# Attention scores in fp32 without an fp16 split, heads always paired, some exponentials kept in SBUF: a fused attention and mixture-of-experts kernel

## The chip, the cores and the metric

The kernel runs on one core of one Trainium2 chip. The metric is device time in microseconds (us). Three timed runs of the kernel before gave a median of 1721.32 us (1719.0 to 1721.88). One more execution was recorded by the hardware profiler; all rows below come from it.

## The reference

Rotary attention feeds a dense mixture of experts with a Sinkhorn-normalised gate:

```python
B, H, S, D = 4, 8, 576, 64
q_rot, k_rot = rotate(q), rotate(k)                  # half = 32, cos/sin tables [S, 32]
scores = (1/sqrt(D)) * q_rot @ k_rot.T
scores -= max(scores, -1); attn = exp(scores)
attn /= sum(attn, -1) + 1e-9
x = (attn @ v) as [2304, 512]
P = exp(x @ w_gate - max); 8 times: normalise rows, then columns
out = sum over 8 experts of P[:, e] * (relu(x @ w1[e]) @ w2[e])   # 512 -> 1024 -> 512
```

## The kernel before

The 32 heads form 16 pairs: one head on partitions 0 to 63, the other on 64 to 127. A stage of attention over the 16 pairs comes first, with the first blocks of expert 0 slipped between; then a short stage with the gate, the Sinkhorn rounds and the rest of expert 0; then experts 1 to 7 as one long stream of matmuls (line 1096).

Attention, for each pair. POOL rotates q and k (lines 369, 373) and scales them by a power of two (385); DVE finds the largest magnitude first (`qk_max`, 282) and makes the scales (`qk_scale`, 350). ACT rounds to fp16 (`z_hi`, 381), POOL subtracts for a low half (`z_lo`, 391). The result is `Z`, four fp16 pieces, in three buffers. A unit is 128 query rows of one head against 576 keys; a pair has nine (four times two, and one "tail", i = 2, that packs 64 rows of both heads). TensorE (PE) multiplies three fp16 products per unit (`s_mm`, 443) into a PSUM tile of two banks; there are three such tiles (`ps_s`). Then, per unit: DVE takes the row maximum (`m_max`, 447), ACT scales it (451) and takes the exponential in place in PSUM with a row sum (454), DVE inverts the sum (458, 460), ACT writes the high fp16 half (`e_hi`, 463), DVE the low half (`e_lo`, 285), and only then is the PSUM tile free. SP transposes the halves by DMA (479, 475) and PE multiplies with v (`av_mm`, 490); ACT and DVE evacuate x (499, 501).

In the first eight pairs (SOLO = 8) each head's unit has score matmuls of its own; in the last eight the two heads' matmuls alternate. `Plan` orders the work: every operation has an engine, a due time (AT, SH1), a cost (US), dependencies and buffers. `Plan.run` plays these through and emits each engine's instructions in that fixed order; semaphores hold them back on the chip. Expert 0's chunks (F1, line 624; F2, line 645) have late due times, so on PE they fill gaps. They may be placed before the end of attention for three of five blocks (E0_IN); the rest waits for the score tiles' PSUM (`rel`).

Of the kernel before, what the change touches and what calls it, by code (L numbers as in the profile page):

```python
# [9 lines left out]
F32 = mybir.dt.float32  # L10
# [8 lines left out]
P = 128  # L19
# [24 lines left out]
SOLO = 8  # L44
# [5 lines left out]
E_TOP = 10  # L50
# [165 lines left out]
def attention_moe(ctx, tc, qk, v, trigs, eye, wg, w1, w2, out):  # L216
# [79 lines left out]
    trig = att.tile([P, 2, S], F32, name="trig")  # L296
# [50 lines left out]
    def qk_scale(p):  # L347
        s, inv = pow2_of(raw[p][2][:, 0:2], 2, 14, "p")
        c = small.tile([P, 1], F32, tag="pc", bufs=4, name="pc")
        dve.tensor_scalar(c, inv[:, 0:1], 1.0 / math.sqrt(D), inv[:, 1:2], op0=ALU.mult, op1=ALU.mult)  # L350
        sc[p] = (c, s)

    def qk_max(p):
        mx = small.tile([P, 2], BF16, tag="pmx", name="pmx")
        absmax(mx, raw[p][0])
        raw[p].append(mx)

    def qk_gmax(p):

        ps = ps_g.tile([P, 512], F32, tag="g", name="g")  # L360
        pe.matmul(ps[:, 0:2], neg, raw[p][2], start=True, stop=True)
        raw[p][2] = ps

    def rope_mult(e, p, n, t):
        r = raw[p][n]
        if t is None:
            engine[e].tensor_tensor(r, r, trig[:, n, :].unsqueeze(1).to_broadcast([P, 2, S]), op=ALU.mult)
        else:
            engine[e].tensor_tensor(r[:, t, :], r[:, t, :], trig[:, n, :], op=ALU.mult)
# [5 lines left out]
    def z_hi(p, t):  # L375
        if p not in Z:
            Z[p] = att.tile([P, 4, S], F16, tag="Z", bufs=ZB, name="Z")
        if p == 0:
            hi_of(Z[p][:, 2 * t, :], raw[p][0][:, t, :], sc[p][1][:, t : t + 1])
        else:  # L380
            act.copy(Z[p][:, 2 * t, :], raw[p][0][:, t, :])

    def z_scale(p, t, e):
        x = raw[p][0][:, t, :]
        engine[e].tensor_scalar(x, x, sc[p][1][:, t : t + 1], None, op0=ALU.mult)

    def z_lo(p, t, e="dve"):
        if p == 0:
            stt_lo(Z[p][:, 2 * t + 1, :], raw[p][0][:, t, :], sc[p][1][:, t : t + 1], Z[p][:, 2 * t, :])
        else:  # L390
            engine[e].tensor_tensor(Z[p][:, 2 * t + 1, :], raw[p][0][:, t, :], Z[p][:, 2 * t, :], op=ALU.subtract)
        if t == 1:
            del raw[p]

    def prep0():

        qk_max(0)
        qk_gmax(0)
        for t in range(2):
            rope_mult("dve", 0, 0, t)  # L400
        qk_scale(0)
        rope_mult("pool", 0, 1, 1)
        rope_mult("dve", 0, 1, 0)
# [25 lines left out]
    def s_mm(n, ps, js):  # L429

        p, i = divmod(n, 5)
        zz = Z[p]
        for j in js[:1] if i == TAIL else js:
            ps[j] = ps_s.tile([P, 2, 512], F32, tag="s", name="s")
        for x, y in ((0, 2), (1, 2), (0, 3)):
            for kh in range(2):
                for j in js:
                    r = HEADS[j]
                    if i == TAIL:
                        o, q = ps[0][r, kh, 0:HS], zz[r, x, 256:320]  # L440
                    else:
                        o, q = ps[j][:, kh, 0:HS], zz[r, x, QT[i] : QT[i] + P]
                    pe.matmul(o, q, zz[r, y, QH[kh]], start=(x, y) == (0, 2), stop=(x, y) == (0, 3))  # L443
# [5 lines left out]
    def e_exp(p, ps, b):  # L449
        c = small.tile([P, 1], F32, tag="nb", bufs=4, name="nb")  # L450
        act.activation(c, b[0], AF.Copy, bias=E_TOP * math.log(2.0), scale=sc[p][0])
        b.append(small.tile([P, 1], F32, tag="es", bufs=4, name="es"))
        e = ps[:, :, 0:HS]
        act.activation(e, e, AF.Exp, bias=c, scale=sc[p][0], accum_out=b[1])

    def e_inv(b):
        t = small.tile([P, 1], F32, tag="et", bufs=2, name="et")
        dve.tensor_scalar(t, b[1], 2.0**-N_TOP, 1e-9 * 2.0 ** (E_TOP - N_TOP), op0=ALU.mult, op1=ALU.add)
        b.append(small.tile([P, 1], F32, tag="ei", bufs=6, name="ei"))
        dve.reciprocal(b[2], t)  # L460

    def e_hi(n, ps, b):
        act.activation(ets[n % NEB][:, 0, 0:S].rearrange("p (a b) -> p a b", a=2), ps[:, :, 0:HS], AF.Copy, scale=b[2])  # L463

    def e_lo(n, ps, b):
        h, l = (ets[n % NEB][:, x, 0:S].rearrange("p (a b) -> p a b", a=2) for x in range(2))
        stt_lo(l, ps[:, :, 0:HS], b[2], h)
# [185 lines left out]
    def batch_logits(b):  # L653
# [3 lines left out]
        raw=2, Z=ZB, S=3, G=2, E=NEB, ET0=1, ET1=1, vraw=1, vhl=2, hA=1, hB=1, raw0=1, pc=4,  # L657
# [33 lines left out]
    def pair_ops(p):  # L691
# [7 lines left out]
        rw, z = ("raw", p), ("Z", p)  # L699
        if p > 0:  # L700
            add("ld", "sp", "ld", lambda: load_qk(p), allocs=[rw])
            add("mx", "dve", "mx", lambda: qk_max(p), ["ld"], uses=[rw])
            g = ("G", f"q{p}")
            add("gm", "pe", "gm", lambda: qk_gmax(p), ["mx"], allocs=[g])
            add("sc", "dve", "sc", lambda: qk_scale(p), ["gm"], allocs=[("pc", p)], uses=[g])
            for t, x in enumerate("qk"):
                add("z" + x, choice("ts", "tsd"), 0, lambda e, t=t: z_scale(p, t, e), ["a" + x, "sc"], uses=[rw])
                add("c" + x, choice("pro", "tt"), 0, lambda e, t=t: rope_mult(e, p, 0, t), ["mx"], uses=[rw])
                add("s" + x, choice("pro", "tt"), 0, lambda e, t=t: rope_mult(e, p, 1, t), ["ld"], uses=[rw])
                add("a" + x, choice("ad_p", "ad"), 0, lambda e, t=t: rope_add(p, t, e), ["c" + x, "s" + x], uses=[rw])  # L710
            add("hq", "act", "hi", lambda: z_hi(p, 0), ["zq"], allocs=[z], uses=[rw])
            add("hk", "act", "hi", lambda: z_hi(p, 1), ["zk", "hq"], uses=[z, rw])
            add("lq", choice("ptt", "tt"), 0, lambda e: z_lo(p, 0, e), ["hq"], uses=[z, rw])
            add("lk", choice("ptt", "tt"), 0, lambda e: z_lo(p, 1, e), ["hk", "lq"], uses=[z, rw])
        for h in range(2):
            plan.add(f"et{h}.{p}", ("none", 0.0), at["TR"], lambda: None, allocs=[(f"ET{h}", p)])
        for i in range(5):
            n, ps = 5 * p + i, {}
            solo = p < SOLO and i != TAIL
            for js in ((0,), (1,)) if solo else ((0, 1),):  # L720
# [3 lines left out]
                    ([f"lk.{p}"] if p else []) + before, allocs=[("S", (n, j)) for j in (js[:1] if i == TAIL else js)] + ([z] if n == js[0] == 0 else []),  # L724
                    uses=[z],
                )
                before[:] = [name]
            for j in range(1 if i == TAIL else 2):
                u, bb = 2 * i + j - (i > TAIL), []
                m = 9 * p + u  # L730
                pt, e = ("S", (n, j)), ("E", m)
# [698 lines left out]
```

## Time and profile before

| | |
|---|---|
| median of 3 runs | 1721.32 us |
| profiled execution | 1726.83 us, span 1725.0 us |
| last attention output (line 501) starts | 459.69 us |
| first matmul of experts 1 to 7 | 556.97 us |
| busy share of the span | PE 92%, DVE 81%, ACT 65%, POOL 40% |

The span runs from the first to the last instruction; 1.83 us of the profiled time lie around it. A busy share is an average over three stages that differ, so the rows below are taken by stage. PEclk is the granted TensorE clock as a share of full speed (2.4 GHz).

### The profile page before, as it was taken

What the parts mean: (1) busy time and instruction counts of PE and PEld (TensorE: products, weight loads), DVE (VectorE), ACT (ScalarE), POOL (GpSimd) and SP (SyncE); (2) the same over time, 40 slices, a digit from 0 to 9 for tenths busy, and PEclk for the clock granted to TensorE, in tenths of its full rate; (3) what the DMA queues carried; (4) which work ended last, traced back from release to release, by engine and by line L of the source; (5) the groups of instructions that cost most, each with busy time, mean ns of one, the idle gap of its engine ahead of it and who ended that gap; (6) DMA issues with size and microseconds to landing.
All of it is one profiled execution on the core that took longest, in us unless ns stands there. A gap on an engine that the chain in (4) does not pass through costs nothing.

```text
span 1725.0 us, 36197 instructions
## 1 busy us (share of the span) xinstructions
PE 1595.5 (92%) x14206; PEld 1271.9 (74%) x14206; DVE 1400.3 (81%) x2834; ACT 1119.5 (65%) x2320; POOL 693.6 (40%) x564
## 2 busy tenths in 40 slices
PE   3777776879999899999999999999999999999998
PEld 1444433444445798989898989898998989898987
DVE  7778876776698788888888888888888888887877
ACT  5678777677434866666666666666676666666643
POOL 5989879820135222223332322333232332332310
PEclk9856778899999999999999999999999999999999
DMA  8798977868412355646465556464655655555543
GB/s 259 147 192 188 226 157 142 176 102 121 94 55 94 116 153 139 153 122 164 117 156 130 146 129 159 113 158 123 155 131 145 136 146 149 142 143 131 135 115 95
DMA packets 243131, 243.67 MB, mean 141 GB/s; under 512 B 195600, under 2 KB 195728, under 8 KB 238864
## 3 DMA queue, kind: packets, MB, share of 16 engines
q1 hardware_dynamic: 224240, 180.01, 38.9%
q0 software_dynamic: 18720, 61.35, 19.9%
q8 instruction: 111, 1.82, 0.4%
q14 instruction: 60, 0.49, 0.1%
HBM read 123.36 MB, written 9.44 MB: 77 GB/s over the span
## 4 chain that ended last, share of the span: by engine, by line
PE 70%; DVE 2%; ACT 1%; issue 1%; POOLq 0%; DVEq 0%
PE m L1096 65%; PE g L645 3%; PE g L624 2%; ACT accA L883 0%; DVE prob L868 0%; DVE prob L859 0%; DVE hl L635 0%; ACT h L1137 0%; ACT accB L883 0%; DVE cs L866 0%; DVE accB L1159 0%; DVE u L1148 0%; PE g L490 0%; DVE h L1141 0%; DVE ts L916 0%
## 5 line engine op out<-in xcount | busy, mean ns | idle before, releaser
L1096 PE MATMUL m<-w2h,h 128*128 128x256 f16 x3528 | 627.2, 273 | 3.3 <-DVE accB L1159 1.5
L1096 PEld LDWEIGHTS <-h 128*128 128x128 f16 x5292 | 515.3, 98 | 63.5 <-issue 2.0
L1096 PE MATMUL m<-w2l,h 128*128 128x256 f16 x1764 | 480.8, 273 | 0.0
L1096 PEld LDWEIGHTS <-w1h 128*128 128x128 f16 x3920 | 369.2, 98 | 39.9 <-issue 3.0
L1096 PE MATMUL m<-ts,w1h 128*128 128x256 f16 (+1 forms) x2240 | 347.6, 262 | 2.7 <-ACT m L1119 1.3
L1161 ACT ACTIVATE ev<-m,pp 128x256 f32<-128x256 f32 x468 | 198.0, 468 | 186.2 <-PE m L1096 185.2
L1096 PE MATMUL m<-ts,w1l 128*128 128x256 f16 (+1 forms) x1120 | 284.0, 262 | 0.0
L1096 PE MATMUL m<-xx,w1h 128*128 128x256 f16 (+1 forms) x1680 | 261.4, 262 | 0.0
L1046 POOL TENSOR_TENSOR wraw<-wraw 128x512 f32<-128x512 f32 x112 | 160.7, 1435 | 176.1 <-issue 133.4
L1141 POOL TENSOR_TENSOR h<-u,h 128x512 f16<-128x512 f32 (+1 forms) x70 | 78.2, 1117 | 356.2 <-ACT h L1137 356.2
L1096 PE MATMUL m<-xx,w1l 128*128 128x256 f16 (+1 forms) x840 | 213.1, 262 | 0.0
L1096 PEld LDWEIGHTS <-w1l 128*128 128x128 f16 x1960 | 191.8, 98 | 17.8
L443 PE MATMUL s<-Z 64*128 64x288 f16 (+1 forms) x960 | 139.1, 361 | 65.3 <-DVE et L285 42.7
L1159 DVE SCALAR_TENSOR_TENSOR ev<-m,pp,ev 128x256 f32<-128x256 f32 x351 | 154.7, 478 | 45.4 <-ACT ev L1161 28.3
L443 PEld LDWEIGHTS <-Z 64*128 64x128 f16 (+1 forms) x960 | 70.4, 117 | 144.5 <-DVE et L285 60.6
L1137 ACT ACTIVATE h<-m 128x512 f16<-128x512 f32 (+1 forms) x210 | 120.4, 574 | 44.2 <-PE m L1096 40.7
L447 DVE TENSOR_REDUCE nm<-s 128x1 f32<-128x576 f32 x144 | 104.4, 752 | 44.2 <-PE s L443 43.4
L1122 DVE TENSOR_TENSOR u<-m,u 128x512 f32<-128x512 f32 (+1 forms) x140 | 88.9, 635 | 55.0 <-PE m L1096 29.2
L1137 ACT ACTIVATE h<-u 128x512 f16<-128x512 f32 (+1 forms) x210 | 122.4, 586 | 14.8 <-DVE u L1148 11.1
L285 DVE SCALAR_TENSOR_TENSOR et<-s,ei,et 128x576 f16<-128x576 f32 x144 | 114.0, 812 | 15.2 <-ACT et L463 14.8
L1119 ACT COPY u<-m 128x512 f32<-128x512 f32 (+1 forms) x140 | 75.9, 542 | 71.4 <-PE m L1096 70.4
L1170 POOL DMA_DIRECT2D accA<-ev x78 | 69.0, 1021 | 126.5 <-ACT ev L1161 108.4
(148 smaller groups left out, 2727.4 us busy)
## 6 DMA issues: line engine op xcount, KB each, us to landing
ts<-xd SPq DMA_DIRECT2D x110, 512.0 KB, 3.9
accA<-ev POOLq DMA_DIRECT2D x78, 512.0 KB, 5.9
wraw<-in_w SPq DMA_DIRECT2D x28, 1024.0 KB, 5.0
raw<-in_qk SPq DMA_DIRECT2D x32, 576.0 KB, 4.9
accB<-ev POOLq DMA_DIRECT2D x26, 512.0 KB, 7.3
ts<-xd SPq DMA_DIRECT2D x28, 256.0 KB, 2.9
accB<-ev POOLq DMA_DIRECT2D x26, 256.0 KB, 3.3
vraw<-in_v SPq DMA_DIRECT2D x4, 1280.0 KB, 7.2
```

What stands on the lines that cost most here:

```text
L285: dve.scalar_tensor_tensor(lo, x, s, hi, op0=ALU.mult, op1=ALU.subtract)
L443: pe.matmul(o, q, zz[r, y, QH[kh]], start=(x, y) == (0, 2), stop=(x, y) == (0, 3))
L447: dve.tensor_reduce(b[0], ps[:, :, 0:HS], axis=AX.XY, op=ALU.max, negate=True)
L1046: put(k, "pool", US["ptt"], lambda: pool.tensor_tensor(quad(o), quad(x), quad(y), op=op), deps, uses=[raw])
L1096: pe.matmul(live[bank][:, f_ * width : (f_ + 1) * width], step(x, i, f_), y[:, i], start=first and f_ == 0 and n == 0, stop=n == 5, skip_g ...
L1119: act.copy(live[n], live[src])
L1122: dve.tensor_tensor(live[n], live[x], live[n], **add)
L1137: act.activation(t[:, 0:cols], live[src], func)
L1141: engine[eng].tensor_tensor(l, live[src], h, **sub)
L1159: dve.scalar_tensor_tensor(o, x, s, o, op0=ALU.mult, op1=ALU.add)
L1161: act.activation(o, x, AF.Copy, scale=s)
L1170: pool.dma_start(out=a, in_=ev[th][:, 0:nt], accum_op=ALU.add)
```

## The change

Rotated q and k are no longer split. The score matmuls take the fp32 rows, once per unit and key half. The factor 1/8 goes into a second table `trigq` for q. Row maximum, exponential and sum need no scale any more. All pairs alternate heads (SOLO = 0). In units 0, 2, 5 and 7 of nine (`EU`) the exponentials go to one of four fp32 tiles in SBUF (`e32`), so their PSUM tile is free after the exponential; the five others stay in PSUM as before. Three rotated x tiles (`rx`) replace the three `Z`. The planner's costs change with it (`s` 0.9 to 1.3, `s8` 0.76 to 1.1, `ex`, `eh`, `tsv`, `tsw` up, `plv`, `plw` down); due times stay.

```diff
-SOLO = 8
+SOLO = 0
+EU = (0,2,5,7)
+E32 = 4
...
     def s_mm(n, ps, js):
-        zz = Z[p]
+        x = raw[p][0]
...
-        for x, y in ((0, 2), (1, 2), (0, 3)):
-            for kh in range(2):
-                for j in js:
...
-                    pe.matmul(o, q, zz[r, y, QH[kh]], start=(x, y) == (0, 2), stop=(x, y) == (0, 3))
+        for kh in range(2):
+            for j in js:
...
+                pe.matmul(o, q, x[r, 1, QH[kh]], start=True, stop=True)
...
-        c = small.tile([P, 1], F32, tag="nb", bufs=4, name="nb")
-        act.activation(c, b[0], AF.Copy, bias=E_TOP * math.log(2.0), scale=sc[p][0])
...
-        act.activation(e, e, AF.Exp, bias=c, scale=sc[p][0], accum_out=b[1])
+        if out:
+            b.append(att.tile([P, 2, HS], F32, tag="e32", bufs=E32, name="e32"))
+        act.activation(b[2] if out else e, e, AF.Exp, bias=b[0], accum_out=b[1])
...
-            add("mx", "dve", "mx", lambda: qk_max(p), ["ld"], uses=[rw])
-            add("gm", "pe", "gm", lambda: qk_gmax(p), ["mx"], allocs=[g])
-            add("sc", "dve", "sc", lambda: qk_scale(p), ["gm"], allocs=[("pc", p)], uses=[g])
...
-            add("hq", "act", "hi", lambda: z_hi(p, 0), ["zq"], allocs=[z], uses=[rw])
...
+                sb = u in EU
+                p2 = ("e32", m) if sb else pt
```

On DVE, in a late pair of the kernel before, a round of two units (score tiles s_3768 and s_3769) stands like this; `nm` is the maximum, `et_`/`ei_` the inverse, line 285 the low half:

```order
L447 TENSOR_REDUCE nm_3788<-s_3768 128x1
L447 TENSOR_REDUCE nm_3795<-s_3769 128x1
L282 TENSOR_REDUCE vmx_3804<-vraw_3666 128x1
L458 TENSOR_SCALAR et_3818<-es_3799 128x1
L460 RECIPROCAL ei_3820<-et_3818 128x1
L282 TENSOR_REDUCE vmx_3804<-vraw_3666 128x1
L458 TENSOR_SCALAR et_3831<-es_3816 128x1
L460 RECIPROCAL ei_3833<-et_3831 128x1
L285 SCALAR_TENSOR_TENSOR et3_101<-s_3768,ei_3820,et3_101 128x576
L282 TENSOR_REDUCE vmx_3804<-vraw_3666 128x1
L285 SCALAR_TENSOR_TENSOR et4_102<-s_3769,ei_3833,et4_102 128x576
L447 TENSOR_REDUCE nm_3875<-s_3853 128x1
```

The next round's maximum (s_3853) comes after both low halves of this one. On DVE of the changed kernel, in a middle pair, rounds s_2717/s_2718 and s_2777/s_2778:

```order
L402 TENSOR_REDUCE nm_2741<-s_2717 128x1
L402 TENSOR_REDUCE nm_2749<-s_2718 128x1
L415 TENSOR_SCALAR et_2773<-es_2758 128x1
L417 RECIPROCAL ei_2775<-et_2773 128x1
L415 TENSOR_SCALAR et_2784<-es_2771 128x1
L417 RECIPROCAL ei_2786<-et_2784 128x1
L402 TENSOR_REDUCE nm_2793<-s_2777 128x1
L402 TENSOR_REDUCE nm_2797<-s_2778 128x1
L592 SCALAR_TENSOR_TENSOR hl_2668<-g_2702,hh_2667 128x512
L285 SCALAR_TENSOR_TENSOR et1_100<-s_2718,ei_2786,et1_100 128x576
```

The next round's maxima now come ahead of the low half of s_2718. Over the whole order a round's first maximum stands ahead of the last low half of the round before it in 66 of 79 cases; before it was 37 of 40 in pairs 0 to 7 and 8 of 39 in pairs 8 to 15.

On PE of the kernel before, the start of one paired round of scores (12 matmuls, each with a weight load):

```order
L443 LDWEIGHTS Z_3469
L443 MATMUL s_4140<-Z_3469 128x288
L443 LDWEIGHTS Z_3469
L443 MATMUL s_4141<-Z_3469 128x288
L443 LDWEIGHTS Z_3469
L443 MATMUL s_4140<-Z_3469 128x288
L443 LDWEIGHTS Z_3469
L443 MATMUL s_4141<-Z_3469 128x288
```

And the end of one in the changed kernel, three of its four fp32 matmuls, with the first rows of the multiplication by v behind them:

```order
L398 MATMUL s_2718<-raw_2117 128x288
L398 MATMUL s_2717<-raw_2117 128x288
L398 MATMUL s_2718<-raw_2117 128x288
L447 LDWEIGHTS vv_2425
L447 MATMUL g_2727<-ET_105,vv_2425 64x288
```

A round has 4 matmul rows in place of 12, and an fp32 one has no weight load of its own in the program. In PE's whole order, ahead of the last multiplication by v stood 261 of 480 F1 matmuls and 192 of 432 F2; now 225 and 192.

## Rows read from the trace of the kernel before

**Rows 1.** The page's chain that ended last, shares of the span by line.
```profile
PE m L1096 65%; PE g L645 3%; PE g L624 2%; ACT accA L883 0%; DVE prob L868 0%; DVE prob L859 0%; DVE hl L635 0%; ACT h L1137 0%; ACT accB L883 0%; DVE cs L866 0%; DVE accB L1159 0%; DVE u L1148 0%; PE g L490 0%; DVE h L1141 0%; DVE ts L916 0%
```

**Rows 2.** Windows: pairs 1-7, pairs 8-14, stage after attention, experts; columns in first line.
```profile
core 0: us, PE busy (x) PEld busy (x) DVE busy (x) ACT busy (x) POOL busy (x), PEclk, DMA share, GB/s
38.50:228.30 189.80, 139.69 (x956) 77.41 (x953) 146.85 (x357) 141.56 (x311) 170.83 (x120) 0.71 0.92 192
228.30:426.30 198.00, 157.16 (x1248) 79.42 (x1247) 141.00 (x335) 143.95 (x320) 115.21 (x80) 0.89 0.73 135
...
460.00:558.00 98.00, 95.42 (x542) 49.73 (x542) 89.97 (x165) 35.47 (x68) 44.28 (x32) 1.00 0.15 56
558.00:1725.00 1167.00, 1157.52 (x11165) 1042.34 (x11162) 972.29 (x1870) 757.61 (x1535) 339.55 (x304) 1.00 0.54 137
```

**Rows 3.** Waits in 38.5 to 426.3: who for whom, us, times, longest.
```profile
PEld L443 <- DVE et L285: 51.5, 41, 3.7
...
DVE nm L447 <- PE s L443: 40.5, 47, 4.6
```

**Rows 4.** Timeline of one round in pair 15: start, us, engine, line, operation.
```profile
426.31 1.41 DVE L447 TENSOR_REDUCE nm<-s 128x1 f32<-128x576 f32 x2
427.42 0.81 ACT L454 ACTIVATE s<-s,nb,pc 128x576 f32<-128x576 f32 x1
...
430.15 1.54 DVE L285 SCALAR_TENSOR_TENSOR et<-s,ei,et 128x576 f16<-128x576 f32 x2 [0.28 <-ACT et L463]
...
430.80 1.14 PE L443 MATMUL s<-Z 64*128 64x288 f16 x12
...
431.85 0.76 DVE L447 TENSOR_REDUCE nm<-s 128x1 f32<-128x576 f32 x1 [0.16 <-PE s L443]
```

**Rows 5.** Timeline: first maximum, last attention output, first expert matmuls.
```profile
13.56 0.76 DVE L447 TENSOR_REDUCE nm<-s 128x1 f32<-128x576 f32 x1 [0.63 <-PE s L443]
...
459.69 0.46 DVE L501 SCALAR_TENSOR_TENSOR xx<-g,xx 128x288 f16<-128x288 f32 x1 [3.03 <-ACT xx L499]
...
556.97 0.38 PE L1096 MATMUL m<-xx,w1h 128*128 128x256 f16 x2
```

**Rows 6.** Timeline around an fp32 matmul (line 862), and its weight loads' durations (min/median/max).
```profile
483.70 0.38 PE L645 MATMUL g<-wh,hl 128*128 128x512 f16 x1
483.70 0.41 PEld L862 LDWEIGHTS g<-prob,ones 128*128 128x128 f32 x2
483.92 0.41 PE L862 MATMUL g<-prob,ones 128*128 128x144 f32 x2
484.16 0.38 PE L645 MATMUL g<-wh,hh 128*128 128x512 f16 x1
...
L862 PEld LDWEIGHTS g<-prob,ones x16: 186/190/190, 469.9 to 505.3; 128*128 128x128 f32 x16
```

**Rows 7.** Groups of instructions in 14 to 460: busy us, mean ns, idle before.
```profile
L451 ACT ACTIVATE nb<-nm,pc 128x1 f32<-128x1 f32 x144 | 41.6, 289 | 79.6 <-DVE nm L447 79.2
L282 DVE TENSOR_REDUCE pmx<-raw 128x2 bf16<-128x1152 f32 x15 | 20.1, 1337 | 0.0
L381 ACT CAST Z<-raw 128x576 f16<-128x576 f32 x30 | 19.3, 672 | 5.9 <-PE s L443 3.6 <-POOL raw L385 2.2
L276 DVE TENSOR_SCALAR inv<-e 128x1 f32<-128x1 f32 x37 | 4.3, 150 | 0.8
L350 DVE TENSOR_SCALAR pc<-inv 128x1 f32<-128x1 f32 x15 | 3.0, 199 | 0.9 <-ACT s L454 0.9
```

**Rows 8.** Line 285 by tile: instructions, duration ns min/median/max, first and last start.
```profile
L285 DVE SCALAR_TENSOR_TENSOR et<-s,ei,et x144: 797/809/822, 18.5 to 452.1; 128x576 f16<-128x576 f32 x144
L285 DVE SCALAR_TENSOR_TENSOR w1l<-wraw,s,w1h x98: 741/746/1765, 483.4 to 1594.2; 128x512 f16<-128x512 f32 x98
L285 DVE SCALAR_TENSOR_TENSOR w2l<-wraw,s,w2h x98: 737/746/1754, 528.3 to 1629.7; 128x512 f16<-128x512 f32 x98
```

More of the change, by code (lines that the diff above doesn't have):

```diff
@@ L293, in attention_moe @@
     engine = dict(pool=pool, dve=dve)
-    trig = att.tile([P, 2, S], F32, name="trig")
+    trig, trigq = (att.tile([P, 2, S], F32, name=n) for n in ("trig", "trigq"))
     idt = att.tile([P, P], BF16, name="idt")
@@ L300, in attention_moe @@
     ET = att.tile([P, 2, 10, S], F16, name="ET")
-    raw, vraw, Z, vhl, sc, vs, vmx, avp = ({} for _ in range(8))
+    raw, vraw, vhl, vs, vmx, avp = ({} for _ in range(6))
     def load_qk(p):
-        raw[p] = [att.tile([P, 2, S], F32, tag=t, bufs=2, name="raw") for t in ("rx", "ry")]
+        raw[p] = [att.tile([P, 2, S], F32, tag=t, bufs=k, name="raw") for t, k in (("rx", ZB), ("ry", 2))]
         for n in range(2):
@@ L345, in v_ctok @@
             act.activation(dst, src, AF.Copy, scale=inv[rows])
[L347 to L362, printed above, removed]
-    def rope_mult(e, p, n, t):
[L365 to L369, printed above, removed]
+    def rope_mult(e, p, n, t):
+        x = raw[p][n][:, t, :]
+        engine[e].tensor_tensor(x, x, (trig if t else trigq)[:, n, :], op=ALU.mult)
     def rope_add(p, t, e="dve"):
@@ L373, in rope_add @@
         engine[e].tensor_tensor(x[:, t, :], x[:, t, :], y[:, t, :], op=ALU.add)
[L375 to L393, printed above, removed]
-    def prep0():
[L397 to L403, printed above, removed]
+    def prep0():
+        c = 1.0 / math.sqrt(D)
+        x, y = raw[0]
+        dve.scalar_tensor_tensor(x[:, 0], x[:, 0], c, trig[:, 0], op0=ALU.mult, op1=ALU.mult)
+        dve.tensor_tensor(x[:, 1], x[:, 1], trig[:, 0], op=ALU.mult)
+        pool.tensor_tensor(y[:, 1], y[:, 1], trig[:, 1], op=ALU.mult)
+        dve.scalar_tensor_tensor(y[:, 0], y[:, 0], c, trig[:, 1], op0=ALU.mult, op1=ALU.mult)
         rope_add(0, 0)
-        z_hi(0, 0)
         rope_add(0, 1)
-        z_lo(0, 0)
-        z_hi(0, 1)
-        z_lo(0, 1)
+        act.activation(trigq, trig, AF.Copy, scale=c)
     def v_hi(p):
@@ L431, in s_mm @@
         p, i = divmod(n, 5)
[L432 removed]
+        x = raw[p][0]
         for j in js[:1] if i == TAIL else js:
             ps[j] = ps_s.tile([P, 2, 512], F32, tag="s", name="s")
[L435 to L443 removed]
+        for kh in range(2):
+            for j in js:
+                r = HEADS[j]
+                if i == TAIL:
+                    o, q = ps[0][r, kh, 0:HS], x[r, 0, 256:320]
+                else:
+                    o, q = ps[j][:, kh, 0:HS], x[r, 0, QT[i] : QT[i] + P]
+                pe.matmul(o, q, x[r, 1, QH[kh]], start=True, stop=True)
     def m_max(ps, b):
@@ L447, in m_max, with e_exp, e_hi, e_lo @@
         dve.tensor_reduce(b[0], ps[:, :, 0:HS], axis=AX.XY, op=ALU.max, negate=True)
-    def e_exp(p, ps, b):
-        c = small.tile([P, 1], F32, tag="nb", bufs=4, name="nb")
-        act.activation(c, b[0], AF.Copy, bias=E_TOP * math.log(2.0), scale=sc[p][0])
+    def e_exp(ps, b, out):
         b.append(small.tile([P, 1], F32, tag="es", bufs=4, name="es"))
         e = ps[:, :, 0:HS]
-        act.activation(e, e, AF.Exp, bias=c, scale=sc[p][0], accum_out=b[1])
+        if out:
+            b.append(att.tile([P, 2, HS], F32, tag="e32", bufs=E32, name="e32"))
+        act.activation(b[2] if out else e, e, AF.Exp, bias=b[0], accum_out=b[1])
+        if not out:
+            b.append(e)
     def e_inv(b):
         t = small.tile([P, 1], F32, tag="et", bufs=2, name="et")
-        dve.tensor_scalar(t, b[1], 2.0**-N_TOP, 1e-9 * 2.0 ** (E_TOP - N_TOP), op0=ALU.mult, op1=ALU.add)
+        dve.tensor_scalar(t, b[1], 1e-9, 2.0**-N_TOP, op0=ALU.add, op1=ALU.mult)
         b.append(small.tile([P, 1], F32, tag="ei", bufs=6, name="ei"))
[L460 to L465, printed above, removed]
+        dve.reciprocal(b[3], t)
+    def e_hi(n, b):
+        act.activation(ets[n % NEB][:, 0, 0:S].rearrange("p (a b) -> p a b", a=2), b[2], AF.Copy, scale=b[3])
+    def e_lo(n, b):
         h, l = (ets[n % NEB][:, x, 0:S].rearrange("p (a b) -> p a b", a=2) for x in range(2))
-        stt_lo(l, ps[:, :, 0:HS], b[2], h)
+        stt_lo(l, b[2], b[3], h)
     def e_turn(n):
@@ L656, in attention_moe @@
     plan = Plan(dict(
-        raw=2, Z=ZB, S=3, G=2, E=NEB, ET0=1, ET1=1, vraw=1, vhl=2, hA=1, hB=1, raw0=1, pc=4,
+        rx=ZB, ry=2, e32=E32, S=3, G=2, E=NEB, ET0=1, ET1=1, vraw=1, vhl=2, hA=1, hB=1, raw0=1,
         G1=4, H=2, stg=1,
@@ L723, in pair_ops @@
                     name, ("pe", US["s8" if i == TAIL or solo else "s"]), at["S"] + 2 * i, lambda n=n, ps=ps, js=js: s_mm(n, ps, js),
-                    ([f"lk.{p}"] if p else []) + before, allocs=[("S", (n, j)) for j in (js[:1] if i == TAIL else js)] + ([z] if n == js[0] == 0 else []),
-                    uses=[z],
+                    ([f"aq.{p}", f"ak.{p}"] if p else []) + before, allocs=[("S", (n, j)) for j in (js[:1] if i == TAIL else js)] + ([rx] if n == js[0] == 0 else []),
+                    uses=[] if n == js[0] == 0 else [rx],
                 )
@@ L1312, in attention_moe @@
     act.activation(warm, ones[:, 0:1], AF.Exp)
-    raw[0] = [att.tile([P, 2, S], F32, tag=t, bufs=2, name="raw") for t in ("rx", "ry")]
+    raw[0] = [att.tile([P, 2, S], F32, tag=t, bufs=k, name="raw") for t, k in (("rx", ZB), ("ry", 2))]
     sp.dma_start(out=raw[0][0], in_=qk[0, :, 0])
```

43 lines of the change are left out of this document (18 added, 25 removed).

## The prediction

> **What bounds the kernel now.** I read the chain of waits first: 65% of the span is the expert stream on line 1096, which the change does not touch [rows 1]. The windows by stage show where it can act. From 558 on PE is busy 1157.5 of 1167 us at full clock: that stage stays. Between 460 and 558 PE is busy 95.4 of 98 us, with what attention left of expert 0. In attention nothing is full: DVE is busy 146.9 of 189.8 us (77%) in pairs 1 to 7 and 141.0 of 198.0 (71%) in pairs 8 to 14, ACT 75% and 73%, POOL 90% and 58%; PE's mean granted clock there is 0.71 and 0.89 of full speed, a mix of the 1.2 and 2.4 GHz levels [rows 2]. So attention is bound by a loop of waits. The list of waits names it: PE's weight loads for scores waited 51.5 us for DVE's low halves, which free the PSUM tiles, and DVE's maxima 40.5 us for PE's scores [rows 3].
>
> The timeline of one round shows that loop: maxima from 426.31, first exponential at 427.42, low halves from 430.15 to 431.69, and only then, at 431.85, the next maximum; its scores (12 matmuls in 1.14 us) had started at 430.80, while the low halves ran [rows 4]. The pitch is (426.31 - 13.56) / 15 = 27.5 us a pair, and attention ends at 459.7 [rows 4, 5].
>
> **The change part by part.** *Scores on PE.* No score matmul in fp32 stands in the trace; the nearest is line 862, with 144 columns. Its two records start at 483.92, and the next fp16 matmul at 484.16: 0.24 us for two passes, 0.12 each [rows 6]. With 288 columns a pass is 0.24 us, a matmul 0.48. A round has 4 matmuls, 8 passes. Fp16 heads on the two halves of the array run beside each other: 12 matmuls of 288 columns at 0.12 us would take 1.44 us in a row, and took 1.14 with their drain [rows 4]. If fp32 does the same, in order, each head's second pass runs beside the other's first: five slots, 1.2 us, and 0.25 of drain, 1.45 us at 2.4 GHz against 1.14. Without overlap it is 8 x 0.24 + 0.25 = 2.2; at 1.2 GHz the two are 2.7 and 4.1. I take 1.45 at full clock, as the row of the same two heads is the nearer one. In pairs 0 to 7, where a head's six matmuls stood alone, 12 cost about 1.44 us in a row already, so PE's work in attention stays about the same.
>
> [...] Line 862's second weight load of 0.19 us costs nothing visible: two passes fit in 0.24 us on the same rows of the array [rows 6]. [...]
>
> *The PSUM tile's hold.* Four of nine units free their tile after the exponential. Maximum start to end of that exponential was 427.42 + 0.81 - 426.31 = 1.92 us with the scaling step of 0.29 [rows 4, 7]; without it 1.63. Before, both tiles of a round were held for 431.69 - 426.31 = 5.4 us. So with the third tile the next scores can start 1.6 us after a round's maxima instead of at 5, and their 1.45 us fall under work of this round. That cover is what the change buys; where DVE's order puts the next maxima behind the low halves all the same (13 of 79 rounds) the round still loses only the wait, not the chain. Next late in such a round is DVE itself.
>
> *ACT.* 144 scalings of 0.289 us go (41.6 us) and 30 casts (19.3 us) [rows 7]. Two scalings per round are on the chain: 0.57 us.
>
> *DVE.* 15 maxima over q and k (20.1 us), and for each pair some 0.8 us of small steps of 0.15 to 0.20 us [rows 7]: 2.1 us a pair. Mean busy was (146.9 + 141.0) / 14 = 20.6 us a pair [rows 2], so 18.5 remain. 64 low halves now read two SBUF operands. From PSUM that took 0.81 us, never over 0.82; the like with both operands in SBUF (w1l, w2l, 512 wide) has a median of 0.75 us but a largest of 1.77 [rows 8], which I read as waits for POOL. Bounds: 0 and 64 x 1.0 = 64 us; as the median is nearer than the largest, I take 0.2 us each, 0.8 us a pair: 19.3.
>
> *POOL* loses its scalings and subtractions; it was ahead of attention and is no term, except that it collides less. *SP* issues the same loads and transposes; three x tiles stand where three Z stood. ACT's exponentials and high halves on e32 I cost as those on PSUM.
>
> *What goes the other way.* 36 F1 matmuls stand behind attention that stood inside, counted in PE's order. One takes 0.22 us there (483.70 to 483.92) [rows 6]: 8 us, on the path, as PE is full in that stage.
>
> *The new pitch, two ways.* By the chain: a round of 5.4 - 0.57 = 4.8 us, four rounds 19.3, plus a tail unit of about 2: 21.3. The same sum for the late pairs before is 4 x (5.4 + 1.05) + 0.7 = 26.5, with 1.05 from the scores' start at 430.80 to the maximum at 431.85 [rows 4]; the measured pitch there is 198.0 / 7 = 28.3 [rows 2], 1.8 more for stray waits. With these: 23.1. By DVE: 19.3 us at 77% would be 25.1, at the 83% that DVE reaches in the expert stage (972 of 1167) [rows 2] 23.2. I take 23.3.
>
> *The sum.* 15 x (27.5 - 23.3) = 63 us. The last pair, 33.4 us from its first maximum to the end [rows 4, 5], saves 4 more. The start saves about 1 (pair 0's maximum and split go, but its second load still comes late). So 68 us off attention, 8 given back: span 1725.0 - 60 = 1665, profiled 1667. The profiled run lies 5.5 us above the median of the runs, so I forecast a median of 1661 us.
>
> **The rivals.** *First, the other sign: fp32 passes of the two heads don't overlap.* Then a round's scores take 2.2 us, 4.1 at the lower clock; at the windows' mean clock of about 0.8 (some 40% of the time at half speed) 3.0. PE then carries each pair 5 rounds x 3.0 of scores, 7 us of the other attention matmuls and 8 of expert 0 at that clock (estimated from 157.2 us of PE in 7 pairs, less the scores): 30 us, in order. It becomes the bound and the pitch about 30: 16 x 2.5 + 8 = 48 us lost, median 1769. It decides from a pitch of 27.0 on, where 16 x 0.5 just pays for the 8. For it: no row shows fp32 on half the array. Against it: fp16 does it on the same rows.
>
> *Second, the transposes and loads.* The DMA share was 0.92 in pairs 1 to 7 and 0.73 in pairs 8 to 14 [rows 2]: 24.9 and 20.7 us of engine time a pair, unchanged by the edit. If these can't be packed closer, pairs 1 to 7 stop at about 25.5 and the rest at 23.3: mean 24.3, a gain of 16 x 3.2 + 1 - 8 = 44 us, median 1677. For it: the share is already high. Against: in those rows little waits for DMA.
>
> *Third, weight loads in the open.* Each pass costs 0.19 + 0.24: five slots 2.15 us. It hides in rounds that are bound by DVE, and adds up to 0.7 us x 5 in others. Taking half, the pitch is 25: median 1688. Rows 6 speak against it.
>
> *Fourth, the loop closes better:* no stray waits, pitch 21.3: 16 x 6.2 + 1 - 8 = 92 us, median 1629.
>
> *Fifth, nothing comes of it:* DVE's order keeps its waits and the hold is traded for queueing; pitch 27, no change.
>
> **How the numbers follow.** Forecast, with pitches of 22.3 to 24.3 or the second rival: 0.60, and its own range 1642 to 1680. Fourth rival 0.13. Third, or the collisions with POOL at several times my value: 0.14, 1680 to 1715. First 0.10. Fifth 0.03. A measurement of this kernel can tell about 0.2%, 3.4 us, from no change. Faster: 0.60 + 0.13 + 0.14 = 0.87; same 0.03; slower 0.10. The range of 8 in 10 leaves out the first rival and the far end of the fourth: 1620 to 1712.
>
> **What would show it.** Score passes of the two heads starting while the other's runs, 0.24 us apart at full clock, and a round's scores near 1.45 us; next scores starting within 2 us of a round's maxima; maxima waiting far less than 40 us for PE; the last attention output near 392; the experts' first matmul near 497, 105 us behind it; a DMA share near 1 in the early pairs. A pitch above 27 or passes in single file make it wrong, and so does a stage after attention that grows by much more than 8 us.

## The result, and the profile after

The changed kernel takes 1694.36 us (median of five runs, 1692.77 to 1696.53). Its ratio to the kernel before is 0.9844, 95% interval 0.9822 to 0.9865. The forecast was 1661 us: the sign came, and 27 us of the forecast 60. The time lies inside the stated range of 1620 to 1712, far above the forecast itself.

The profiled execution is that of 1694.36 us, span 1692.3. Stage ends first (timeline of DVE and PE; they answer to [rows 5]):

```profile
13.27 1.42 DVE L402 TENSOR_REDUCE nm<-s 128x1 f32<-128x576 f32 x2 [2.24 <-PE s L398]
...
419.53 0.46 DVE L458 SCALAR_TENSOR_TENSOR xx<-g,xx 128x288 f16<-128x288 f32 x1 [3.19 <-ACT xx L456]
...
524.22 0.38 PE L1046 MATMUL m<-xx,w1h 128*128 128x256 f16 x2
```

Attention ends 40.2 us earlier, where 68 were forecast. The stage behind it grew from 97.3 to 104.7 us, by 7.4 where 8 were forecast. So of the span's forecast gain 28 us are missing, all in attention. (In the median 33 are missing: the forecast took off 5.5 us by which the profiled run of before lay above its median, and the profiled run of after is the median itself.) Its windows, pairs 1 to 7, pairs 8 to 14 and the two later stages (columns as in [rows 2]):

```profile
32.10:233.40 201.30, 134.88 (x898) 74.80 (x899) 147.09 (x322) 118.13 (x246) 138.81 (x94) 0.87 0.82 176
233.40:389.50 156.10, 134.32 (x976) 72.25 (x974) 124.02 (x292) 109.62 (x231) 74.29 (x49) 0.93 0.92 177
420.00:524.00 104.00, 102.05 (x567) 52.25 (x567) 90.82 (x167) 36.27 (x68) 43.06 (x32) 1.00 0.22 81
524.00:1692.00 1168.00, 1158.76 (x11174) 1043.39 (x11172) 972.47 (x1870) 758.47 (x1537) 339.92 (x304) 1.00 0.53 136
```

Late pairs fell from 28.3 to 22.3 us (156.1 / 7), better than the forecast 23.3, and the DMA share there rose from 0.73 to 0.92. Early pairs stood at 28.8 (201.3 / 7) where they had taken 27.1. From one pair's first maximum to the next one's the pitches were 18.8, 36.3, 19.6, 33.1, 39.9, 20.0, 23.2, 29.3, 20.0, 22.3, 26.0, 27.2, 21.1, 19.6 and 19.9 us, in the mean 25.1. Nine pairs run at the forecast pitch or below, and six take 26 to 40. So the question is what those six wait for.

The waits in attention (who for whom, us, times, longest) answer to [rows 3]:

```profile
DVE nm L402 <- PE s L398: 56.7, 37, 10.0
PE g L447 <- DMA ET<-et: 41.3, 18, 11.0
PEld L447 <- DMA ET<-et: 23.6, 11, 8.3
ACT et L420 <- DMA ET<-et: 21.9, 13, 4.5
PEld s L398 <- DVE et L285: 11.6, 4, 7.5
```

The wait that the change was meant to take away has shrunk to 11.6 us (weight loads of the scores for low halves, 51.5 us before [rows 3]). In its place PE's multiplication by v waits for transposed tiles. Over the whole of attention in the kernel before, the same waits were small:

```profile
PEld L490 <- DMA ET<-et: 12.1, 8, 3.7
PE g L490 <- DMA ET<-et: 11.8, 11, 4.0
ACT et L463 <- DMA ET<-et: 5.1, 5, 2.1
```

One such stall, pair 3, on the timeline: SP's issues, PE, and DVE (the brackets give the idle time before a row and what ended it):

```profile
92.23 0.53 SPq L310 DMA_DIRECT2D vraw<-in_v  x1
92.86 13.34 SPq L436 DMA_TRANSPOSE ET<-et  x6
...
90.22 1.24 PE L398 MATMUL s<-raw 64*128 64x288 f32 x8 [0.99 <-ACT e L409]
102.42 2.37 PE L447 MATMUL g<-ET,vv 128*64 128x288 f16 x18 [10.96 <-DMA ET<-et]
104.72 2.19 PE L398 MATMUL s<-raw 64*64 64x288 f32 x8
...
96.44 0.82 DVE L285 SCALAR_TENSOR_TENSOR et<-s,ei,et 128x576 f16<-128x576 f32 x1
106.96 0.76 DVE L402 TENSOR_REDUCE nm<-s 128x1 f32<-128x576 f32 x1 [9.70 <-PE s L398]
```

SP issues a v load of 1280 KB, and issuing the six transposes behind it takes 13.3 us. For 3.6 of these SP waits for low halves; the last low half before the stall's end is done at 97.3 (96.44 + 0.82), and from there to 102.4 only transfers are left, 5 us. PE's next row in its fixed order is the multiplication by v, which needs them: 10.96 us of standing. The scores behind it show no wait of their own, but stand behind it in the order; so DVE has no maxima for 9.70 us. The granted clock was 0.99 in 91.4 to 94.4 and 0.50 in 94.4 to 102.4, while PE stood. The tail unit's scores at 104.72 take 2.19 us, where those of two later tail units (239.69, 260.43) take 1.19 at a granted clock of 1.00; here it is 0.50 (1.07 is the window's DMA share):

```profile
104.70:106.90 2.20, 2.20 (x12) 0.82 (x12) 0.00 (x0) 0.00 (x0) 0.00 (x0) 0.50 1.07 204
```

The second pattern is on DVE. ACT's high half and DVE's low half of pair 4's first unit, one of the four in SBUF:

```profile
123.94 0.77 ACT L420 ACTIVATE et<-e,ei 128x576 f16<-128x576 f32 x1 [0.56 <-ACT s L409]
...
150.63 1.61 DVE L285 SCALAR_TENSOR_TENSOR et<-e,ei,et 128x576 f16<-128x576 f32 x1
```

The low half's input was there at 124.7 (123.94 + 0.77), and it ran at 150.6. The line that adds `el` has a new `lock=sb`: by it the planner places the low half of an SBUF unit only where POOL is idle. In DVE's order the low half of unit 0 stands 13 rows behind its inverse on average (at most 38) and that of unit 2 12 (37); before it was 5 and 6 (at most 14). Their transposes follow that late.

### The profile page after: what moved, and what is told of

It is laid out like the page before. It is cut to its first block, busy times and chain, and to the rows that moved or that the text cites. A ratio compares the mean times of both kernels' runs of the same rounds, so it can differ in the third digit from the quotient of the medians.

```text
span 1692.3 us, 35046 instructions
## 1 busy us (share of the span) xinstructions
PE 1575.3 (93%) x13870; PEld 1267.0 (75%) x13870; DVE 1375.2 (81%) x2736; ACT 1054.7 (62%) x2145; POOL 617.0 (36%) x504
## 4 chain that ended last, share of the span: by engine, by line
PE 72%; DVE 2%; ACT 1%; issue 1%; POOLq 0%; DVEq 0%
PE m L1046 66%; PE g L581 3%; PE g L602 2%; ACT accA L833 0%; DVE prob L809 0%; ACT h L1087 0%; ACT accB L833 0%; DVE accB L1109 0%; DVE u L1098 0%; DVE rs L807 0%; DVE ts L866 0%; DVE hl L592 0%; PE g L447 0%; DVE h L1091 0%; DVE u L887 0%
## 5 line engine op out<-in xcount | busy, mean ns | idle before, releaser
L1046 PEld LDWEIGHTS <-w1h 128*128 128x128 f16 x3920 | 369.2, 98 | 39.9 <-issue 3.0
L1109 DVE SCALAR_TENSOR_TENSOR ev<-m,pp,ev 128x256 f32<-128x256 f32 x351 | 154.8, 478 | 45.3 <-ACT ev L1111 28.3
L398 PE MATMUL s<-raw 64*128 64x288 f32 (+1 forms) x640 | 134.1, 500 | 50.3 <-ACT e L409 20.9
L398 PEld LDWEIGHTS s<-raw 64*128 64x128 f32 (+1 forms) x640 | 69.3, 204 | 101.0 <-issue 27.7
L447 PE MATMUL g<-ET,vv 128*64 128x288 f16 x960 | 82.5, 321 | 50.7 <-DMA ET<-et 41.3
L447 PEld LDWEIGHTS <-vv 128*64 128x64 f16 x960 | 60.2, 122 | 79.5 <-issue 48.9
```

Of the source, the lines that this page charges most:

```text
L398: pe.matmul(o, q, x[r, 1, QH[kh]], start=True, stop=True)
L447: pe.matmul(po[r], x[:, j, jt, :], e[:, j, 5 * n + jt, :], start=jt == 0 and x is vh and n == 0, stop=jt == 4 and n == 1,)
L1046: pe.matmul(live[bank][:, f_ * width : (f_ + 1) * width], step(x, i, f_), y[:, i], start=first and f_ == 0 and n == 0, stop=n == 5, skip_g ...
L1109: dve.scalar_tensor_tensor(o, x, s, o, op0=ALU.mult, op1=ALU.add)
```

## The experiments

All are edits of the changed kernel unless it says otherwise; `e1` is e1_lowhalf_free_order. Ratios are to the kernel before, with 95% intervals. Theory A: low halves late by order. B: DMA time for transposes and loads. C: the order as a whole. D: collisions with POOL. E: the work on v and w.

**e1_lowhalf_free_order**

```diff
-lambda m=m, b=bb: e_lo(m, b), [f"eh.{m}"], uses=[e, p2], lock=sb)
+lambda m=m, b=bb: e_lo(m, b), [f"eh.{m}"], uses=[e, p2])
```

> The changed kernel, but the planner no longer holds the low halves of the four SBUF units back until POOL is idle. In DVE's order the low half of unit 0 then stands 5 rows behind its inverse on average (at most 8) where it stood 13 (at most 38), unit 2 the same (5 against 12), units 5 and 7 at 5 against 9. Theory A, late low halves: the transposes come earlier, PE waits less for transposed tiles (41 us before attention's end in the changed kernel), the pitch goes from 25.1 to about 23.3 us a pair and the time to about 1667 us (1655 to 1682). Rival D, collisions with POOL: these low halves now run while POOL runs; their mean goes from 1.04 us to 1.3 or more, and the time stays at 1690 to 1710. Rival B, transposes and loads are too slow by themselves: no change, 1690 to 1698.

1681.38 us (0.9765, 0.9744 to 0.9787), 13 us below the changed kernel. Attention ends at 412.1, and the first expert matmul starts at 511.9 for 524.2. The waits in attention, and the SBUF low halves (count, duration ns min/median/max, first and last start):

```profile
DVE nm L402 <- PE s L398: 49.6, 37, 5.6
PE g L447 <- DMA ET<-et: 37.6, 19, 6.9
PEld L447 <- DMA ET<-et: 34.2, 15, 7.0
ACT et L420 <- DMA ET<-et: 6.8, 7, 2.0
...
L285 DVE SCALAR_TENSOR_TENSOR et<-e,ei,et x64: 797/818/2057, 18.1 to 401.6; 128x576 f16<-128x576 f32 x64
```

Theory A holds for half of what it claimed. ACT's waits for transposes, which free the `et` buffers, fell from 21.9 to 6.8 us, and PE's longest stall from 11.0 to 6.9; but PE's and its weight loads' waits for transposed tiles (which may overlap) come to 72 us, no less than the 65 without the edit. Of the 12.3 us, 7.4 are in attention; 4.9 are in the stage behind it, since this order also has 24 more F1 matmuls inside attention (249 for 225; 24 x 0.22 = 5.3). (A second profile of the same program, e10 below, ends attention at 407.7: such an end holds to some 4 us.) Rival D falls: the low halves took 1.08 us in the mean, as against 1.04.

**e2_no_sbuf_units**

```diff
-EU = (0,2,5,7)
+EU = ()
```

> The changed kernel with no unit's exponentials in SBUF: fp32 scores, no scale and paired heads alone. Its maxima stand behind all low halves of the round before in DVE's order. By the prediction's chain a late pair takes 4 x (5.4 - 0.57 + 1.05) + 0.7 + 1.8 = 26.0 us, so 16 x (27.5 - 26.0) - 8 = 16 us gained: about 1705 us (1695 to 1715). Theory A says the SBUF units' own late low halves eat a good part of what they bring, so it would stand within 15 us of the changed kernel. Rival C, the order as a whole: without these units the pairs are even, and the time is at or below that of the changed kernel, 1685 to 1695.

1745.41 us (1.0138, 1.0113 to 1.0163): slower than the kernel before, a clear miss of my 1705, with a pitch of 29.0. Theory A had it within 15 us of the changed kernel and rival C at or below it; both missed too. With pairing, the SBUF units are worth 51 us even with their late low halves.

**e3_pairing_alone** (the kernel before, one constant)

```diff
-SOLO = 8
+SOLO = 0
```

> The kernel before with the heads of all sixteen pairs alternating, nothing else. In the kernel before pairs 8 to 14, which alternate already, took 28.3 us each and pairs 1 to 7 27.1 us. If alternating costs what this difference says, 8 x 1.2 = 10 us are lost: 1731 us; if the difference is due to other work in those pairs, 1721 us within 4. A gain of over 10 us would say that pairing carries the change's gain.

1758.33 us (1.0217, 1.0191 to 1.0243): alternating heads alone costs 36 us, over three times what the late pairs of the kernel before suggested. The planner's order changed with it: a round's first maximum stands ahead of the last low half of the round before in 19 of 79 cases, where it was 45. PE and its weight loads waited for low halves here:

```profile
PEld L443 <- DVE et L285: 98.9, 54, 5.6
PE s L443 <- DVE et L285: 76.5, 47, 5.3
```

**e4_no_pairing**

```diff
-SOLO = 0
+SOLO = 8
```

> The changed kernel with the heads of pairs 0 to 7 apart, as in the kernel before. A head's two fp32 matmuls alone take four passes of 0.24 us in a row, 0.96 us, so a round of two heads 1.92 instead of 1.2: 8 pairs x 4 rounds x 0.72 = 23 us more PE time, of which some lies under other work. But the first head's maximum can start 0.96 us after the scores' start instead of 1.2. I expect 1702 us (1690 to 1715). If pairing is what lets these pairs run at 20 us, it goes to 1710 or more; if the stalls come from the low halves alone (theory A; their order here is as late as in the changed kernel, 12.5 rows for unit 0), it stays within 8 us of it.

1709.85 us (0.9929, 0.9906 to 0.9953). Attention ends at 414.2, earlier than in the changed kernel, with a pitch of 24.7, yet the stage behind it takes 128.2 us where it took 104.7: in PE's order 192 F1 and 129 F2 matmuls stand ahead of the last multiplication by v, for 225 and 192. Here pairing pays by the room that it leaves for expert 0, not as pitch. Theory A had it within 8 us of the changed kernel; it is 15 us off.

**e9_fp32_alone**

```diff
-SOLO = 0
-EU = (0,2,5,7)
+SOLO = 8
+EU = ()
```

> The changed kernel with neither of its two other parts: fp32 scores without scale, heads apart in pairs 0 to 7, no unit in SBUF. Known so far: the kernel before 1721 to 1723 us; pairing alone on it 1758; fp32 and pairing 1745; fp32 and SBUF units 1710; all three 1694. If the parts add up, fp32 alone is 1745 - 36 = 1709 us, and the SBUF units would then be worth nothing without pairing. If the SBUF units are worth their 51 us in either setting, fp32 alone is 1760.

1719.73 us (0.9986, 0.9975 to 0.9997): 0.14% less, next to nothing. Both of my values were missed: the parts don't add up. Beside fp32, pairing alone costs 26 us and SBUF units alone bring 10; with the units pairing brings 15, and with pairing the units bring 51. My reading, argued from the three tiles and the waits of e3, and not tested by itself: alternating scores need both tiles of a round free at once, and only the short hold frees them in time.

**e5_fewer_load_bytes** (from e1)

```diff
+        if b:
+            vraw[b] = vraw[0]
+            sp.dma_start(out=vraw[b][:, 0].rearrange("p j a d -> p (j a d)"), in_=v[b][:, 0:640])
+            return
...
-        for i in range(4):
+        for i in range(4 if n == 1 else 1):
```

> As e1_lowhalf_free_order, order unchanged, but three of the four v loads bring a quarter of their bytes and so does the second w load of expert 0 (4.4 MB less; the tiles keep older values there, so the output is another one). In e1 the slow pairs stand where these loads run: v issued at 80.8, 183.6 and 277.9 us, w at 111; pairs 3, 7, 11 and 4 took 28.0, 31.0, 28.2 and 32.3 us against a median of 23.0. Theory B, the DMA engines are what these pairs wait for: 1280 KB took 6.4 us from issue to landing, so 4.4 MB are about 22 us; these pairs fall to 24 to 26, and the time to 1661 us (1655 to 1668). Theory E, the work on v and w (maxima on DVE, casts on ACT, subtractions on POOL), which stays: 1677 to 1685.

1669.89 us (0.9697, 0.9681 to 0.9714): 11.5 us less. Pairs 7 and 11 fell from 31.0 and 28.2 to 25.9 and 25.8, pairs 3 and 4 only from 28.0 and 32.3 to 27.1 and 30.5. That lies between the two ranges: theory B, at half of its size.

**e6_half_transposes** (from e1; the tail unit's alike, and zeros at the start where the high halves stood in ET)

```diff
-        x = ets[n % NEB].rearrange("p n a -> p (n a)")
+        x = ets[n % NEB][:, 1, :]
...
-            sp.dma_start_transpose(out=ET[:, k % 2, :, at : at + P], in_=x)
+            sp.dma_start_transpose(out=ET[:, k % 2, 5:10, at : at + P], in_=x)
```

> As e1_lowhalf_free_order, order unchanged, but only the low halves are transposed: each transpose moves 640 columns instead of 1280 (the multiplication by v runs on zeros for the high halves, so the output is another one). A transpose took 1.69 us in e1, ten a pair. Theory B: about 8 us of DMA time a pair go, the pitch falls from 24.7 to about 21 us, and the time to 1625 us (1615 to 1645). Theory E or the order of the work as the limit: the transposes land a little earlier, nothing else: 1670 to 1682.

1656.11 us (0.9619, 0.9604 to 0.9635): 25 us less, all of it in attention, which ends at 385.9 with a pitch of 23.1. The windows of attention, e1 and then this kernel:

```profile
14.00:412.00 398.00, 324.45 (x2145) 174.08 (x2145) 309.27 (x694) 259.02 (x539) 231.51 (x154) 0.90 0.89 180
```

```profile
14.00:388.00 374.00, 321.82 (x2195) 173.42 (x2195) 308.89 (x697) 259.01 (x540) 233.67 (x157) 0.91 0.57 130
```

The engines do the same work; only the DMA share fell, from 0.89 to 0.57. That is 398 x 0.89 - 374 x 0.57 = 141 us of DMA time for half the transposes, so all of them take some 282 of e1's 354. (The halving is an estimate.) The waits fell too, DVE's for scores from 49.6 us, PE's and its weight loads' for transposed tiles from 37.6 and 34.2:

```profile
DVE nm L402 <- PE s L398: 25.7, 32, 3.0
PEld L447 <- DMA ET<-et: 16.4, 8, 5.3
...
PE g L447 <- DMA ET<-et: 14.0, 6, 6.8
```

Theory B had 1625 us, so it has less than half of its size here as well. And the 25 us are an upper bound for it: two of the three products by v now read zeros that no transpose writes, and ACT's waits for the buffers of the high halves (6.8 us in e1) are nearly gone with the edit. e5, which leaves the transposes alone, has no such side.

**e12_short_maxima** (from e1)

```diff
-        absmax(vmx[b][:, c : c + 1], vraw[b][:, c], axis=AX.XYZ)
+        absmax(vmx[b][:, c : c + 1], vraw[b][:, c, 0, 0])
...
-wraw0[n][:, i * 1024 : (i + 1) * 1024])
+wraw0[n][:, i * 1024 : i * 1024 + 64])
```

> As e1_lowhalf_free_order, order unchanged, but the maxima over v and over expert 0's weights read 64 columns instead of 640 or 1024 (scales may differ, the rest of the work stays). With half the transposes the pairs that prepare v and w were still slow (31.0, 26.2, 25.6 us against a median of 21.5), so theory E says DVE's work on them is a cost of its own: 16 x 1.2 + 8 x 1.1 = 28 us of DVE go, half of it on the path: 1667 us (1660 to 1674). If the loads' bytes alone make those pairs slow: 1678 to 1683.

1679.21 us (0.9755, 0.9733 to 0.9776): 15 us of DVE work gone (294.3 for 309.3 us up to attention's end), where I had 28, and 2 us of time, within the spread of e1. Theory E falls for DVE's part; ACT's and POOL's work on v and w was not tried.

**e7_v_in_pieces** (from e1)

```diff
-            plan.add(f"ldv.{b}", ("sp", 10.0), at["ldv"], lambda: load_v(b), allocs=[vr])
+        for c in range(KC):
+            plan.add(f"ldv.{b}.{c}", ("sp", 2.5), at["ldv"], lambda c=c: load_v(b, c), allocs=[(f"vraw{c}", b)])
```

> As e1_lowhalf_free_order with v loaded in four pieces of 320 KB, each as soon as its own quarter of the tile is free, instead of 1280 KB at once; same bytes. If the burst is what stalls a pair, the transposes wait at most a quarter as long behind it: pairs 3, 7 and 11 lose 3 to 5 us each, 1670 us (1664 to 1676). If it is the sum of bytes, or the work on v: 1678 to 1684.

1679.13 us (0.9749, 0.9727 to 0.9771), not told from e1. Attention ends 8.1 us earlier, at 404.0, but 24 fewer F1 matmuls stand inside it, and the stage behind grows by 4.8. PE's and its weight loads' waits for transposed tiles did fall, to 22.4 and 21.0 us.

**e10_av_later** (from e1) and **e11_pieces_av_later** (from e7_v_in_pieces)

```diff
-AV=-19.6
+AV=-15.6
```

> As e1_lowhalf_free_order, with the due time of the multiplication by v four units later (-15.6 for -19.6), so that PE's order has more scores and fewer multiplications by v ahead of transposes that have not landed. In e1 PE waited 37.6 and its weight loads 34.2 us for transposed tiles. If that wait is what stops the scores behind it, half of it goes: 1665 us (1655 to 1675). If the transposes then start later because their target tiles come free later (theory B stays), 1678 to 1690.

> As e7_v_in_pieces (1679 us) with the same later due time of the multiplication by v. Same reasoning: 1664 us (1654 to 1674) if PE's waits for transposed tiles (22 and 21 us there) are what stops scores; 1676 to 1690 if not.

1679.47 us (0.9753, 0.9729 to 0.9777) and 1678.43 us (0.9747, 0.9728 to 0.9766). These two test nothing: with the later due time the planner makes the same order on every engine, so that e10 is the program of e1 and e11 that of e7, instruction for instruction. They are repeats, and show that the same program's medians differ by 1 to 2 us (1681.38 and 1679.47; 1679.13 and 1678.43). Whether an order of PE with the scores ahead of the late multiplications by v would shorten the stalls stays open.

**e13_loads_on_act_queue**, **e14_loads_on_pool_queue** (the same with `pool`), **e15_vw_loads_on_act_queue** (v and w alone), all from e1; the loads of v and w are edited alike

```diff
-            sp.dma_start(out=raw[p][n], in_=qk[p, :, n])
+            act.dma_start(out=raw[p][n], in_=qk[p, :, n])
```

> As e1_lowhalf_free_order (1681 us), same bytes and same planned order, but attention's loads of q and k, v and w are issued by ACT instead of SP, so that they go through another queue than the transposes. In e1 six transposes issued behind the w load of 2 MB took 15.7 us to issue, and PE stood still for 6.9. If transposes are late because they stand behind loads in one queue: they run beside the loads, PE's 38 and 34 us of waits for transposed tiles fall by half, 1668 us (1660 to 1676). If it is the sum of bytes: 1678 to 1690. A load that waits for its tile now holds up ACT's exponentials: that could cost up to 1700.

> As e13, with the loads issued by POOL. A load that waits for its tile holds up only the rotation and preparation on POOL, which run ahead. Queue theory: 1666 us (1658 to 1676). Sum of bytes: 1678 to 1690. If issuing from POOL costs much of POOL's time, the rotations come late and the time goes above 1690.

> As e13, but only the v and w loads (three of 1280 KB and four of 512 KB in attention) move to ACT's queue; q's and k's stay on SP's. With a quarter of these bytes the time was 1670. Queue theory: 1672 us (1666 to 1677), as if these loads were nearly gone for the transposes. Sum of bytes: 1678 to 1686.

1709.67 us (0.9916, 0.9884 to 0.9948), 1699.87 us (0.9870, 0.9830 to 0.9909) and 1679.11 us (0.9747, 0.9731 to 0.9764). Another queue brings no time, and moving all loads is slower; e13 lies above all of its ranges. The DMA queues and issues of e13 in 14 to 400 (share of 16 engines; KB each, median us to landing), then one of its waits:

```profile
q1 hardware_dynamic: 169140, 42.15, 65.1%
q10 hardware_dynamic: 5614, 24.60, 21.3%
...
wraw<-in_w ACTq DMA_DIRECT2D x4, 512.0 KB, 15.7
```

```profile
PE g L447 <- DMA ET<-et: 56.8, 20, 12.8
```

With all loads elsewhere PE waits longer for transposed tiles, and the w loads land after 15.7 us where they took 8.4; but ACT's exponentials stand behind loads there too. e15 is the cleaner case: PE's and its weight loads' waits for transposed tiles fell to 29.5 and 26.0 us, and the time stayed. So a place of their own in the queue gives the transposes no time that can be seen, while fewer bytes to move did bring time (11.5 us in e5, 25 in e6). In e13's trace the loads on the second queue took 21.3% of the same 16 engines.

**e8_eight_sbuf_units** (from e1)

```diff
-EU = (0,2,5,7)
+EU = (0,1,2,3,5,6,7,8)
```

> As e1_lowhalf_free_order with the exponentials of eight of nine units in SBUF (all but the tail) on the same four tiles. Without such units the time was 1745 us, with four 1681. If the hold of the PSUM tiles still decides, four more units bring a part of that, 1665 us (1655 to 1675); their low halves cost 64 x 0.27 = 17 us more of DVE, which is not full. If the hold is no longer the limit (theories B or E): 1680 to 1695, since low halves stand 9 rows behind their inverses again, where e1 had 5, and four fp32 tiles for eight units make the exponentials wait.

1744.14 us (1.0124, 1.0099 to 1.0149), far above both of my ranges. The scores now wait for exponentials, and the high halves for `et` buffers:

```profile
PEld s L398 <- ACT e L409: 98.4, 59, 6.0
ACT et L420 <- DMA ET<-et: 50.9, 31, 5.9
```

The stage behind attention grew to 144.0 us. Its order differs from e1's in many places, so I cannot say how much is owed to the four tiles and how much to the order.

## Where the prediction was right and where it failed, point by point

- **Scores.** Right, and better than costed. The first round's timeline in a late pair, 8 records for 4 matmuls:

```profile
274.12 0.79 PEld L398 LDWEIGHTS s<-raw 64*128 64x128 f32 x8 [0.42 <-issue]
274.12 1.24 PE L398 MATMUL s<-raw 64*128 64x288 f32 x8
```

  1.24 us with the drain, where I had 1.45 from [rows 4, 6]: both heads' passes start 7 ns apart, so there are four slots and not five. One head's four records start at 274.119, 274.466, 274.708 and 274.951: 0.24 us apart but for the first. No row of before gave the 0.25 us of drain in my sum; here the last record lasts 0.40 us, 0.16 more than a pass. The first rival (no overlap) and the third (weight loads in the open) fell: the load of that head's third pass lies at 274.467 to 274.654, beside its second pass, on the same rows. With 0.19 us for such a load in the open, the four slots would have taken 4 x (0.24 + 0.19) = 1.7 us. The profile gives the clock as a share of full speed. What I named 2.4 and 1.2 GHz stands in the traces as columns a ns: at 1.00, fp16 matmuls of 512 columns start 0.215 us apart (257.75 to 260.12 in the changed kernel), 2.4 a ns; at 0.50 the fp32 passes of the tail unit at 104.72 stood 0.48 us apart for 0.24 at 1.00, so half of it.
- **The tile's hold.** Right as a mechanism: e2 shows that without it the change loses, and PE's and its weight loads' waits for low halves fell from 42.7 and 60.6 us over attention to 15.3 and 11.6. Late pairs reached 22.3 us.
- **ACT and DVE.** ACT's busy time to attention's end fell from 323.5 to 257.3 us, 66 where I had 61 from [rows 7]. DVE's work came out as summed, (147.1 + 124.0) / 14 = 19.4 us a pair for 19.3. The SBUF low halves cost 1.04 us for 0.81 [rows 8], as I took them (group in 14 to 420: busy us, mean ns, idle before):

```profile
L285 DVE SCALAR_TENSOR_TENSOR et<-e,ei,et 128x576 f16<-128x576 f32 x64 | 66.4, 1039 | 3.9 <-ACT et L420 3.8
```

- **36 F1 matmuls behind attention.** Right: 7.4 us for 8. The last pair: 3.3 us saved for 4; the start: 0.3 for 1.
- **The pitch, 23.3 us.** This step failed; it was 25.1: 15 x 1.8 = 27 of the missing 28 us. The 23.3 needed DVE busy 83% of attention, a share taken from the expert stage; it was 75% (306.3 of 406 us), where 77% would have given my own 25.1. What kept DVE idle were transposes that came late, and two sentences under the step were wrong. "*SP* issues the same loads and transposes" gave DMA no term, because little waited for it in the rows of before. But there 0.82 of 446 us was 366 us of DMA time, and a forecast attention of 378 us (392 - 14) would have needed a share of 0.97. (Attention from 14 us on; a share adds up the packets' times and can pass 1, as the 1.07 above shows, so 0.97 was a warning and no proof.) The second rival had this at a pitch of 24.3 and 1677 us, and I left its chance inside the forecast's; e1, with the order mended, came to 24.7 and 1681, and e6, with less to move, to 23.1 and 1656, with DVE busy 83% (308.9 of 374 us). That fits the chain and the DVE sum for a kernel whose transposes come in time, though two of e6's pairs are still slow.
- **"*POOL* ... is no term, except that it collides less."** Wrong through the planner: the low halves were kept off POOL by standing late. In the changed kernel's trace 20 of the 64 SBUF low halves lasted 0.91 to 2.05 us, all of them beside a POOL instruction; the 31 with none beside them took 0.80 to 0.82, and the 80 from PSUM at most 0.82, 49 of them beside POOL. The collisions cost as much without the planner's rule (e1), with a mean low half of 1.08 us for 1.04, and the rule cost 13 us. My rows showed maxima ahead of low halves, and I read this as the loop opening, not as transposes coming late.

Not settled: why pairs 1 and 4 stay at 28 and 31 us even in e6. Pair 4 (108 to 139 there) holds 7.1 us of F1 matmuls, but also one more wait of PE for transposed tiles, 6.8 us, so part of it is still a stall by transfers. Pair 1 is another case: in the changed kernel (32 to 69) it has 12.1 of the 15.3 us that PE waits for low halves. Nor is it shown what the collisions of low halves with POOL cost in time.

e1 beats both kernels. e7 and e15 stand at 1679, which the repeats of e1 do not tell from it. The rule in the planner is thus 13 to 15 us of the missing gain (e1 and its repeat); for the rest e5 and e6 show that fewer bytes to move bring time back, in the order as it is.

## What to carry to other kernels

When a tightened loop is forecast, multiply the DMA share by the span before and divide by the span you forecast: a quotient near 1 is a warning that transfers come next, however little waits for them now; here it was 0.97, from one case. Look whether an edit of a planner's number changed the order at all before reading its time (e10 and e11 did not). A rule that keeps two engines from colliding can cost more by what it delays than the collisions do. Parts of a change can be worth nothing or less alone (fp32 2 us, pairing -36) and much together, so undo them one at a time before crediting any.

## What the runs showed of the hardware

Fp32 passes of two heads on the two halves of the array ran side by side, 8 records in 1.24 us. A transpose is dear in DMA time: in e13's queues 42.15 MB of mostly transposes took 65.1% of the 16 engines and 24.60 MB of loads 21.3%, 1.8 times as much per byte. Loads on a second queue took their share of the same engines (21.3%), and brought no time. With POOL issuing loads (e14), single low halves on DVE lasted up to 3.9 us, where 2.1 was the longest in e1.
